# Key tails copied by ScalarE instead of GpSimd, and the denominators' tails as 128-row matmuls

## The chip, the cores and the metric

The kernel runs on one core of a Trainium2 chip. The metric is the device time of one execution in microseconds (us). The kernel before takes 469.25 us (median of three runs, 469.03 to 470.44). Engines are named as in the profile: PE (TensorE, with PEld for its weight loads), DVE (VectorE), ACT (ScalarE), POOL (GpSimd) and SP (the engine that issues all DMAs here).

## The reference

An attention with a soft cap is followed by a gated feed-forward block with a spatial gate. All arrays are float32: batch 4, 12 heads, sequence 448, head size 64, model width 768, hidden width 1024.

```python
scores = scale * q @ k.T                       # scale = 1/8, per head
scores = cap * tanh(scores / cap)              # cap = 30
attn = exp(scores - max(scores)); attn = attn / (sum(attn) + 1e-9)
x = attn @ v                                   # heads side by side: (4, 448, 768)
h = gelu_tanh(x @ w_in); u, v = halves of h    # 512 wide each
v = (v - mean) / sqrt(var + 1e-6) * g_ln       # over the 512
v = einsum('ts,bsd->btd', w_sg, v) + b_sg      # over the sequence
out = x + (u * v) @ w_out
```

## The kernel before

**Pairs and chunks.** Two heads make a pair, six pairs a batch, 24 pairs in all. The 448 keys of a head are three chunks of 128 and a tail of 64. A pair is worked in four steps, one per chunk; chunk 0 is the tail, where the 64 keys of both heads lie on the 128 partitions. From the second pair on the order of chunks is 1, 0, 2, 3, so the tail is the second step of a pair.

**A step.** PE makes the scores (L212, or L198 for a tail) as three products of high and low parts, since each float32 operand is split in two roundings (`hl`, hi by L156 or L158, lo by DVE's subtraction L170). ACT takes the tanh out of PSUM (L225) and the exp in place (L228). PE multiplies the exponentials with v (`pav`, L241), and ACT takes the finished pair out (L249). For the tail, the stationary operand `kt` is block-diagonal: the 64 tail keys of head 0 in one block, of head 1 in the other, zero elsewhere, so that one 128-row matmul makes both heads' scores. Two copies per pair (L173, on POOL) fill the two blocks from `hl`; `kt` has one buffer.

**Denominators.** The sum over keys is a matmul with a column of ones (`den`, L261), always two units at once in a flush; each unit is one chunk of both heads. The four results of a flush go to four groups of 32 rows of one PSUM tile. In batch 0 (`ADDS` = 0) every chunk is a unit: 24 units, 12 flushes, 6 of which hold a tail. A tail's two matmuls contract 64 rows each, taken from partitions 0 to 63 and 64 to 127. In batches 1 to 3 DVE first adds the four chunks of a pair (`presum`, L297), and all units have 128 rows.

**The feed-forward work.** While attention of batch b runs, a generator fills in matmuls of batch b-1: normalisation (L334), the gate half (L368), the other half (L412), the spatial gate (L426), the output (L455). Batch 0 has none to fill in. In its place the weights are decoded in batches 0 and 1: 36 pieces of `w_in` and `w_out` arrive by DMA (L553) and are split into high and low parts by a relay, ACT (L563), DVE (L565, L567, L570, L573), POOL (L575), DVE (L580), ACT or DVE (L158, L156) and POOL (L582). The staging tiles are three in `xu`, and spare `raw` tiles later; `w_sg` (L545, L546) needs four pieces more. Every engine takes its own instructions strictly in the order in which they were laid down by the build's scheduler, which moves them against the program's text by its own estimates.

The end of batch 0's attention is read by ACT (L317), and its reciprocal by DVE (L318, L320 to L322) releases the feed-forward work of batch 0, whose first matmuls are L334.

Of the kernel before, what the change touches and what calls it, by code (L numbers as in the profile page):

```python
# [7 lines left out]
FP32 = mybir.dt.float32  # L8
# [4 lines left out]
ACTF = mybir.ActivationFunctionType  # L13
# [41 lines left out]
def kernel(  # L55
# [15 lines left out]
    nc = tc.nc  # L71
    B, NP, _, S = q2.shape
    NC = w_sgT.shape[1]
    FC = S // 128
    TL = S - 128 * FC
# [8 lines left out]
    wp = ctx.enter_context(tc.tile_pool(name="wp", bufs=1))  # L84
# [16 lines left out]
    wsg = [wp.tile([128, NC, S], FP32R, name=f"wsg{s}") for s in range(2)]  # L101
    sel_r = wp.tile([128, NP, 128], FP32R, name="sel_r")
    rds = wp.tile([128, S], FP32R, name="rds")
    ones_sb = wp.tile([128, NP + 31], FP32, name="ones_sb")
    bsg_sb = wp.tile([128, S], FP32, name="bsg_sb")
    g_sb = wp.tile([128, KF], FP32, name="g_sb")
    cap_sb = wp.tile([128, 1], FP32, name="cap_sb")
# [3 lines left out]
    kt = wp.tile([128, 2, 2 * TL], FP32R, name="kt")  # L111

    def f32(ap):
        return ap.bitcast(FP32)
# [18 lines left out]
    def two(t):  # L133
        return t.rearrange("p (a s) -> p a s", a=2)
# [31 lines left out]
    def prep_b(P):  # L166
        if P >= NPAIR:
            return
        hl = qks[P]
        nc.vector.tensor_tensor(out=hl[:, 1], in0=two(raws[P]), in1=f32(hl[:, 0]), op=ALU.subtract)  # L170
        for h in range(2):
            rows = slice(64 * h, 64 * h + 64)
            nc.gpsimd.tensor_copy(out=kt[rows, :, TL * h:TL * h + TL], in_=f32(hl)[rows, :, 1, 128 * FC:])  # L173
        raw_s.put(raws.pop(P))

    def prep_first():
# [53 lines left out]
    def heads(src, c):  # L230
        if c:
            return [two(src)[:, h, :] for h in range(2)]
        return [src[TL * h:TL * h + TL, :S] for h in range(2)]
# [18 lines left out]
    def den(b, units):  # L252
        if b not in den_t:
            den_t[b] = ps_d.tile([128, 512], FP32, tag="den", name="den")
            units_in[b] = 0
        t = den_t[b]
        for half, (P, c, src) in enumerate(units):
            for h, pr in enumerate(heads(src, c)):
                j = 2 * half + h
                lo, n = (0, 128) if c else (TL * h, TL)  # L260
                nc.tensor.matmul(  # L261
                    out=t[32 * j:32 * j + 32, :S],
                    lhsT=ones_sb[lo:lo + n, NP - 1 - P % NP:NP + 31 - P % NP], rhs=pr,
                    start=(units_in[b] < 2), stop=(units_in[b] >= NP * (NC - ADDS[b]) - 2),
                    skip_group_check=True)
            units_in[b] += 1
# [34 lines left out]
    def flush():  # L301
        b, units = flushes.pop(0)
        den(b, units)
        for u in units:
            raw_s.put(u[2])
        if units_in[b] == NP * (NC - ADDS[b]):
            boost[0] = True
            recip(b)
            later(READY_LAG, set_ready)
# [359 lines left out]
    for g in range(NSTEP + LAG + 2):  # L669
        P, c = divmod(g, NC)  # L670
# [13 lines left out]
        if g < NSTEP:  # L684
            soft2(g)
            if c == 0:
                prep_a(P + 1)
            elif c == 1:
                prep_b(P + 1)
                load_pair(P + 2)  # L690
# [92 lines left out]
```

## Time and profile before

| | |
|---|---|
| median of three runs | 469.25 us |
| the profiled execution's own time | 472.69 us |
| its span, first to last instruction | 470.9 us |
| PE, DVE, ACT, POOL busy | 436.7, 335.7, 283.1, 93.0 us |
| mean granted clock of PE | 0.971 |
| POOL's copies into `kt` | 46, 21.9 us |
| `den` matmul instructions (two for each matmul) | 168, of which 24 with 64 rows |

A matmul's busy time is modelled where matmuls are pipelined, and spans on POOL are rough; the distance from one start to the next is the safer reading. The share of an engine over the whole span mixes stages with different limits, so the stages are read apart.

### The profile page before, as it was taken

The page shows a single profiled execution, that of the slowest core. Times are in us where ns is not written, and L with a number is a line of the kernel's source. Part 1 is how long each engine was busy: PE and PEld are TensorE (multiplying, and loading weights), DVE is VectorE, ACT ScalarE, POOL GpSimd, SP SyncE. Part 2 cuts the span into 40 slices and gives each one's busy share as a digit, 9 for nine tenths or more (in the row PEclk, how much of TensorE's full clock was granted, in tenths as well). Part 3 has the DMA queues.
Part 4 walks back from the last instruction along what each step waited for, and adds up shares of the span by engine and source line. Part 5 has one row for each costly group of instructions (what it writes and reads, how often), then busy time and mean ns, then how long its engine had stood idle before and what let it go on. Part 6 is the DMA issues. An engine that isn't in the chain of part 4 may idle for free.

```text
span 470.9 us, 5916 instructions
## 1 busy us (share of the span) xinstructions
PE 436.7 (93%) x2097; PEld 272.5 (58%) x2097; DVE 335.7 (71%) x621; ACT 283.1 (60%) x420; POOL 93.0 (20%) x143
## 2 busy tenths in 40 slices
PE   5997769879999869999999999999999999899996
PEld 2332223337466536675656666666666576678985
DVE  4859866987999896588587457388596355687662
ACT  4776688974686665538578756636777760044310
POOL 0436644301425543110110101000111000001000
PEclk9999979989999959999999999999999999999999
DMA  7563334221421231231210220420200001200002
GB/s 222 198 197 125 114 120 131 90 84 45 126 67 45 90 107 61 100 99 42 63 39 25 61 61 1 141 91 10 63 22 2 22 2 39 78 1 0 1 27 90
DMA packets 20717, 34.18 MB, mean 73 GB/s; under 512 B 3024, under 2 KB 12880, under 8 KB 20688
## 3 DMA queue, kind: packets, MB, share of 16 engines
q1 hardware_dynamic: 20688, 33.81, 22.8%
q8 instruction: 16, 0.26, 0.3%
q14 instruction: 13, 0.11, 0.1%
HBM read 28.30 MB, written 5.51 MB: 72 GB/s over the span
## 4 chain that ended last, share of the span: by engine, by line
PE 70%; DVE 18%; DMA 3%; POOL 3%; ACT 3%; issue 3%; SPq 0%; POOLq 0%; DVEq 0%; ACTq 0%
PE pav L241 14%; PE gp L455 13%; PE gp L368 11%; PE gp L412 10%; PE sc L212 8%; PE gp L426 8%; DVE raw L297 3%; PE den L261 3%; PE sc L198 2%; DMA xu<-in_w_in_dram 2%; DVE xu L580 2%; PE gp L334 1%; POOL xu L575 1%; ACT raw L225 1%; DVE hl L170 1%
## 5 line engine op out<-in xcount | busy, mean ns | idle before, releaser
L225 ACT ACTIVATE raw<-sc,qsc 128x896 f32<-128x896 f32 (+1 forms) x96 | 86.6, 906 | 36.9 <-PE sc L212 19.1
L241 PE MATMUL pav<-raw,v 128*64 128x448 f32 x384 | 94.1, 576 | 1.0 <-ACT xu L249 1.0
L228 ACT ACTIVATE raw<-raw,cap_sb 128x896 f32<-128x896 f32 (+1 forms) x96 | 90.1, 944 | 1.3
L212 PE MATMUL sc<-hl 64*128 64x448 f32 x432 | 69.6, 418 | 15.0 <-ACT raw L225 15.0
L297 DVE TENSOR_TENSOR raw<-raw,raw 64x448 f32<-64x448 f32 (+1 forms) x72 | 63.2, 878 | 6.1 <-PE pav L241 5.1
L368 PE MATMUL gp<-win,r 128*128 128x512 f32 x264 | 65.3, 398 | 1.3 <-DVE t L357 1.0
L212 PEld LDWEIGHTS sc<-hl 64*128 64x128 f32 x432 | 38.5, 195 | 47.2 <-ACT raw L225 21.5
L412 PE MATMUL gp<-r,win 128*128 128x448 f32 x288 | 65.1, 373 | 0.1
L455 PE MATMUL gp<-r,wout 128*128 128x448 f32 x288 | 63.6, 372 | 0.0
L412 PEld LDWEIGHTS gp<-r,win 128*128 128x128 f32 x288 | 52.7, 188 | 14.5 <-issue 9.6
L455 PEld LDWEIGHTS gp<-r,wout 128*128 128x128 f32 x288 | 53.1, 188 | 11.3 <-issue 3.8
L368 PEld LDWEIGHTS gp<-win,r 128*128 128x128 f32 x264 | 48.2, 188 | 19.5 <-issue 5.6
L241 PEld LDWEIGHTS pav<-raw,v 128*64 128x64 f32 x384 | 25.6, 141 | 52.4 <-issue 41.5
L173 POOL CAST kt<-hl 64x128 fp32r<-64x128 f32 x46 | 21.9, 476 | 155.6 <-PE sc L198 111.3
L426 PE MATMUL gp<-wsg,r 128*128 128x448 f32 x176 | 41.5, 382 | 3.4 <-DVE u L357 3.4
L426 PEld LDWEIGHTS gp<-wsg,r 128*128 128x128 f32 x176 | 33.0, 193 | 14.1 <-issue 6.5
L352 DVE SCALAR_TENSOR_TENSOR t<-t,gp 128x448 f32<-128x448 f32 (+1 forms) x28 | 18.0, 644 | 20.5 <-ACT t L351 20.3
L170 DVE TENSOR_TENSOR hl<-raw,hl 128x896 fp32r<-128x896 f32 x23 | 25.8, 1122 | 8.3 <-ACT hl L158 8.1
L382 POOL TENSOR_TENSOR rs<-rs,pw 128x1 f32<-128x1 f32 (+1 forms) x16 | 9.6, 600 | 109.2 <-DVE rs L381 109.1
L460 DVE TENSOR_TENSOR xu<-xu,gp 128x448 f32<-128x448 f32 x24 | 14.6, 612 | 22.6 <-PE gp L455 22.4
L356 ACT ACTIVATE t<-t 128x448 f32<-128x448 f32 (+2 forms) x32 | 19.3, 604 | 16.9 <-DVE t L352 16.9
L261 PE MATMUL den<-raw,ones_sb 128*32 128x448 f32 (+1 forms) x168 | 29.4, 589 | 0.0
(81 smaller groups left out, 463.7 us busy)
## 6 DMA issues: line engine op xcount, KB each, us to landing
v<-in_vp_dram SPq DMA_DIRECT2D x24, 256.0 KB, 3.0
raw<-in_q_dram SPq DMA_DIRECT2D x24, 224.0 KB, 2.6
raw<-in_k_dram SPq DMA_DIRECT2D x24, 224.0 KB, 3.0
xu<-in_w_in_dram SPq DMA_DIRECT2D x21, 256.0 KB, 2.5
out_dram<-xu SPq DMA_DIRECT2D x24, 224.0 KB, 1.9
raw<-in_w_out_dram SPq DMA_DIRECT2D x11, 256.0 KB, 2.7
u<-in_w_sgT_dram SPq DMA_DIRECT2D x4, 224.0 KB, 5.8
raw<-in_w_in_dram SPq DMA_DIRECT2D x3, 256.0 KB, 3.5
```

Of the source, the lines that this page charges most:

```text
L170: nc.vector.tensor_tensor(out=hl[:, 1], in0=two(raws[P]), in1=f32(hl[:, 0]), op=ALU.subtract)
L173: nc.gpsimd.tensor_copy(out=kt[rows, :, TL * h:TL * h + TL], in_=f32(hl)[rows, :, 1, 128 * FC:])
L212: nc.tensor.matmul(out=sc[:, h, :S], lhsT=hl[rows, w, 1, 128 * c - 128:128 * c], rhs=hl[rows, m, 0], start=(i == 0), stop=(i == 2))
L225: nc.scalar.activation(out=prob(g), in_=src, func=ACTF.Tanh, scale=qsc)
L228: nc.scalar.activation(out=prob(g), in_=prob(g), func=ACTF.Exp, scale=cap_sb)
L241: nc.tensor.matmul(out=pav_t[P][64 * h:64 * h + 64, :S], lhsT=w, rhs=two(p_t[g])[:, h if c else 0, :], start=(g % NC == 0), stop=(c == NC ...
L261: nc.tensor.matmul(out=t[32 * j:32 * j + 32, :S], lhsT=ones_sb[lo:lo + n, NP - 1 - P % NP:NP + 31 - P % NP], rhs=pr, start=(units_in[b] < ...
L297: eng.tensor_tensor(out=a, in0=a, in1=w, op=ALU.add)
L368: yield 1, lambda i=i, c=c, a=a, w=w: nc.tensor.matmul(out=ps, lhsT=a[c][:, t * 128:t * 128 + 128], rhs=win[w][:, c, HF:], start=(i == 0), ...
L412: yield 1, lambda a=a, w=w, c=c, st=st, sp=sp: nc.tensor.matmul(out=ps, lhsT=win[w][:, c, f * 128:(f + 1) * 128], rhs=a[c][:, :S], start=s ...
L426: yield 1, lambda i=i, c=c, a=a, w=w: nc.tensor.matmul(out=ps, lhsT=a[c][:, f * 128:(f + 1) * 128], rhs=wsg[w][:, c, :], start=(i == 0), s ...
L455: yield 1, lambda ps=ps, c=c, a=a, w=w, f=f, st=st, sp=sp: nc.tensor.matmul(out=ps, lhsT=wout[w][:, f, c * 128:(c + 1) * 128], rhs=a[f][:, ...
```

## The change

The two copies into `kt` go from POOL to ACT. The tile of ones grows from one plane to three: plane 0 is as before, planes 1 and 2 hold ones for the partitions of head 0 or head 1 alone. A tail's two denominators then contract all 128 partitions of the tail's exponentials, once with plane 1 and once with plane 2, in place of 64 rows each.

```diff
-    ones_sb = wp.tile([128, NP + 31], FP32, name="ones_sb")
+    ones_sb = wp.tile([128, 3, NP + 31], FP32, name="ones_sb")
...
-            nc.gpsimd.tensor_copy(out=kt[rows, :, TL * h:TL * h + TL], in_=f32(hl)[rows, :, 1, 128 * FC:])
+            nc.scalar.activation(
+                out=kt[rows, :, TL * h:TL * h + TL], in_=f32(hl)[rows, :, 1, 128 * FC:], func=ACTF.Copy)
...
-            for h, pr in enumerate(heads(src, c)):
+            for h in range(2):
                 j = 2 * half + h
-                lo, n = (0, 128) if c else (TL * h, TL)
                 nc.tensor.matmul(
                     out=t[32 * j:32 * j + 32, :S],
-                    lhsT=ones_sb[lo:lo + n, NP - 1 - P % NP:NP + 31 - P % NP], rhs=pr,
+                    lhsT=ones_sb[:, 0 if c else 1 + h, NP - 1 - P % NP:NP + 31 - P % NP],
+                    rhs=two(src)[:, h if c else 0, :],
...
-    ones = _np.zeros((128, NP + 31), _np.float32)
-    ones[:, NP - 1::NP] = 1.0
+    ones = _np.zeros((128, 3, NP + 31), _np.float32)
+    ones[:, 0, NP - 1::NP] = 1.0
+    for h in range(2):
+        ones[TL * h:TL * h + TL, 1 + h, NP - 1::NP] = 1.0
```

The scheduler lays the instructions down anew. In the changed program lines after 173 carry a number higher by one. Three places show what moves.

ACT, the end of batch 0's attention, the twelve instructions up to the one that reads the denominators (L317; `raw` are the exponentials' tiles, `win` the decoded weights), before:

```order
L225 ACTIVATE raw_67<-sc,qsc 128x448
L158 ACTIVATE win_117<-xu 128x256
L228 ACTIVATE raw_67<-raw_67,cap_sb 128x448
L225 ACTIVATE raw_69<-sc,qsc 128x896
L158 ACTIVATE win_117<-xu 128x256
L228 ACTIVATE raw_69<-raw_69,cap_sb 128x896
L249 ACTIVATE xu<-pav 128x448
L563 ACTIVATE xu<-xu 128x256 x2
L225 ACTIVATE raw_70<-sc,qsc 128x896
L563 ACTIVATE raw_72<-raw_72 128x256
L228 ACTIVATE raw_70<-raw_70,cap_sb 128x896
L317 ACTIVATE t_102<-den 64x448
```

The same place in the changed program, from the first copy into `kt` of that pair:

```order
L173 ACTIVATE kt<-hl 64x2x64
L229 ACTIVATE raw_67<-raw_67,cap_sb 128x448
L173 ACTIVATE kt<-hl 64x2x64
L226 ACTIVATE raw_69<-sc,qsc 128x896
L158 ACTIVATE win_117<-xu 128x256
L229 ACTIVATE raw_69<-raw_69,cap_sb 128x896
L250 ACTIVATE xu<-pav 128x448
L564 ACTIVATE xu<-xu 128x256 x2
L226 ACTIVATE raw_70<-sc,qsc 128x896
L158 ACTIVATE win_117<-xu 128x256
L229 ACTIVATE raw_70<-raw_70,cap_sb 128x896
L318 ACTIVATE t_102<-den 64x448
```

The copies stand around the tail's exp, one ahead of it and one behind. Over the whole program up to this point ACT has 14 copies more, and 3 fewer of L563 (14 for 17), 3 fewer of L545 (1 for 4) and 1 fewer of L158 (7 for 8): those come later.

DVE, the same end of batch 0, up to the reciprocal (L318 adds the two halves of the denominators, L320 inverts; `hl` is split for the pair to come), before:

```order
L156 CAST hl<-raw_68 128x896
L567 TENSOR_SCALAR raw_72<-raw_72 128x256
L170 TENSOR_TENSOR hl<-raw_68,hl 128x896
L570 SCALAR_TENSOR_TENSOR raw_72<-raw_72 128x256
L580 TENSOR_TENSOR xu<-xu 128x256
L573 TENSOR_SCALAR raw_72<-raw_72 128x256
L318 SCALAR_TENSOR_TENSOR t_102<-t_102,guard,den 64x448
L297 TENSOR_TENSOR raw_77<-raw_77,raw_67 64x448
L320 RECIPROCAL t_102<-t_102 64x448
```

The same place in the changed program:

```order
L156 CAST hl<-raw_68 128x896
L581 TENSOR_TENSOR xu<-xu 128x256
L170 TENSOR_TENSOR hl<-raw_68,hl 128x896
L581 TENSOR_TENSOR xu<-xu 128x256
L568 TENSOR_SCALAR raw_72<-raw_72 128x256
L571 SCALAR_TENSOR_TENSOR raw_72<-raw_72 128x256
L298 TENSOR_TENSOR raw_77<-raw_77,raw_67 64x448
L319 SCALAR_TENSOR_TENSOR t_102<-t_102,guard,den 64x448
L298 TENSOR_TENSOR raw_77<-raw_77,raw_67 64x448
L321 RECIPROCAL t_102<-t_102 64x448
L574 TENSOR_SCALAR raw_72<-raw_72 128x256
```

Ahead of the addition DVE now has 19 of L565, L567 and L570 each for 21, 18 of L573 for 21 and 18 of L580 for 19, and one of L297 for none. By the eleventh split of a pair (L170, in batch 1) the counts of decode pieces are the same in both programs again.

PE, the second and third flush of batch 0 (`den`; the tiles `raw_72` to `raw_75` are its units, `raw_75` a tail), before:

```order
L212 MATMUL sc<-hl 128x448 x12
L261 MATMUL den<-raw_72,ones_sb 32x448 x2
L261 MATMUL den<-raw_73,ones_sb 32x448 x2
L241 MATMUL pav<-raw_74,v 64x448 x2
L241 MATMUL pav<-raw_75,v 64x448 x2
L198 MATMUL sc<-hl,kt 128x448 x3
L212 MATMUL sc<-hl 128x448 x6
L261 MATMUL den<-raw_74,ones_sb 32x448 x2
L261 MATMUL den<-raw_75,ones_sb 32x448 x2
```

The same in the changed program:

```order
L213 MATMUL sc<-hl 128x448 x6
L261 MATMUL den<-raw_72,ones_sb 32x448
L213 MATMUL sc<-hl 128x448 x6
L261 MATMUL den<-raw_72,ones_sb 32x448
L261 MATMUL den<-raw_73,ones_sb 32x448 x2
L242 MATMUL pav<-raw_74,v 64x448 x2
L242 MATMUL pav<-raw_75,v 64x448 x2
L199 MATMUL sc<-hl,kt 128x448 x3
L261 MATMUL den<-raw_74,ones_sb 32x448
L213 MATMUL sc<-hl 128x448 x6
L261 MATMUL den<-raw_74,ones_sb 32x448
L261 MATMUL den<-raw_75,ones_sb 32x448 x2
```

In these two flushes one of the four matmuls stands apart from the other three, with scores between them. The other ten flushes of batch 0 keep their four side by side.

## Rows read from the trace of the kernel before

**Rows 1.** Busy time of each engine by stage (start:end, length, then engines)
```profile
0.00:22.20 22.20, 16.92 (x63) 6.38 (x63) 14.44 (x38) 12.19 (x15) 5.66 (x14) 1.00 0.68 207
22.20:96.60 74.40, 58.81 (x323) 22.18 (x322) 56.29 (x116) 58.35 (x90) 34.45 (x51) 0.93 0.41 131
96.60:118.00 21.40, 21.36 (x78) 12.36 (x78) 17.09 (x39) 12.46 (x23) 3.12 (x6) 0.92 0.20 59
118.00:172.50 54.50, 46.63 (x227) 28.56 (x226) 51.64 (x105) 38.55 (x66) 25.88 (x33) 0.93 0.32 94
172.50:410.00 237.50, 236.89 (x1153) 154.59 (x1153) 158.31 (x252) 143.69 (x199) 21.70 (x36) 0.99 0.16 49
```
**Rows 2.** Chain that ended last, pieces: start, length, what
```profile
17.12 1.75 PE den L261 x8
22.68 5.12 DMA xu<-in_w_in_dram
68.53 3.27 PE den L261 x8
172.47 2.98 PE gp L426 x7
```
**Rows 3.** Waits in batch 0 after 22.2 us: total, times, longest
```profile
PE sc L212 <- ACT raw L225: 10.3, 7, 2.2
ACT xu L563 <- DMA xu<-in_w_in_dram: 8.2, 6, 2.3
DVE xu L580 <- POOL xu L575: 7.6, 9, 1.3
```
**Rows 4.** Timeline: flushes without and with a tail
```profile
23.56 0.96 PE L261 MATMUL den<-raw,ones_sb 128*32 128x448 f32 x8
27.71 1.82 PE L261 MATMUL den<-raw,ones_sb 128*32 128x448 f32 x8
28.58 0.14 PEld L261 LDWEIGHTS den<-raw,ones_sb 64*32 64x32 f32 x4 [0.73 <-issue]
46.94 1.72 PE L261 MATMUL den<-raw,ones_sb 128*32 128x448 f32 x8
68.46 3.34 PE L261 MATMUL den<-raw,ones_sb 128*32 128x448 f32 x8
```
**Rows 5.** Timeline of ACT: small instructions and the starts behind them
```profile
8.60 0.19 ACT L660 ACTIVATE guard<-guard 128x1 f32<-128x1 f32 x1
8.69 1.00 ACT L225 ACTIVATE raw<-sc,qsc 128x896 f32<-128x896 f32 x1
...
45.37 0.57 ACT L545 ACTIVATE wsg<-u 128x448 fp32r<-128x448 f32 x1
...
62.46 0.42 ACT L158 ACTIVATE win<-xu 128x256 fp32r<-128x256 f32 x1 [1.30 <-DVE xu L580]
62.78 0.42 ACT L563 ACTIVATE xu<-xu 128x256 f32<-128x256 uint32 x1
```
**Rows 6.** DVE's decode in batch 0: all, and two lines (ns min/median/max)
```profile
22.20:96.60 74.40, 38.12 (x93) 0.93 0.41 131
...
L570 DVE SCALAR_TENSOR_TENSOR xu<-xu x17: 411/444/1237, 28.7 to 85.5; 128x256 int32<-128x256 int32 x17
...
L580 DVE TENSOR_TENSOR xu<-xu x16: 410/505/1347, 30.6 to 89.1; 128x256 f32<-128x256 f32 x16
```
**Rows 7.** POOL's copies into kt (L173) in batch 0: busy and count
```profile
22.20:96.60 74.40, 4.39 (x12) 0.93 0.41 131
```
**Rows 8.** Timeline: a pair's lo part on DVE, its tail's tanh on ACT
```profile
54.63 1.08 DVE L170 TENSOR_TENSOR hl<-raw,hl 128x896 fp32r<-128x896 f32 x1
55.99 0.61 ACT L225 ACTIVATE raw<-sc,qsc 128x448 f32<-128x448 f32 x1
...
103.38 0.62 ACT L225 ACTIVATE raw<-sc,qsc 128x448 f32<-128x448 f32 x1
...
109.71 1.08 DVE L170 TENSOR_TENSOR hl<-raw,hl 128x896 fp32r<-128x896 f32 x1
```

## The prediction

> **What bounds the kernel now.** I read the busy time by stage first, then the chain that ended last, then the waits of the stage that the change touches.
>
> By stage [rows 1], the span falls in three. From 172.5 to 410 us PE is busy 236.9 of 237.5 us: nothing counts there but matmuls, and the change takes none away. From 118 to 172.5 us DVE is busy 51.6 of 54.5 us and sets the pace; PE has holes, its clock falls to the lower level near the end (0.93 on the mean of the stage), and the chain re-enters PE at 172.47 us at half clock, seven matmuls in 2.98 us [rows 2]. Batch 0, up to 96.6 us, has no such owner: after 22.2 us PE, DVE and ACT are busy 58.8, 56.3 and 58.4 of 74.4 us. It is a relay. PE waits 10.3 us for ACT's tanh, ACT 8.2 us for weight DMAs, DVE 7.6 us for POOL's product [rows 3]; the chain of waits runs through all of them. What shortens one link shortens batch 0 only when the next link is not late anyway. Then whatever time batch 0 and the DVE-bound stage save together moves the PE-bound stage forward and comes off the end.
>
> **The denominators' tails.** A flush of eight instructions takes 0.96 us when all have 128 rows, 1.82 us with a tail; at half clock 1.72 and 3.34 us [rows 4]. The four 64-row ones do not run beside the others: their weight load starts 0.73 us late [rows 4], as after a change of shape. With 128 rows and masked ones a tail's flush should take what the others take: 0.86 us less at full clock, 1.6 us at half. Batch 0 has six. Two of them lie on the chain, 1.75 us at 17.12 and 3.27 us at 68.53 [rows 2]; they become 0.9 and 1.75 us: -0.9 and -1.5. For the other four I count nothing, since PE waits for ACT behind them; the bound is -0.86 each. Against this, the second and third flush are torn in two, and the matmul that stands apart may cost what the 64-row group cost, 0.86 us each. Neither is on the chain (which is in a weight DMA from 22.68 us [rows 2]): 0, bound +1.7.
>
> **The copies on ACT.** No row shows a copy of 64x128. After a small ACT instruction the next one starts 0.09 us later (128x1) or 0.32 us later (128x256) [rows 5]; half way by width is 0.21, and I take 0.22 us. Fourteen stand ahead of L317: +3.1 us (1.3 to 4.5). The new order takes away ahead of that point three L563 and one L158 at 0.32, and three L545 at 0.47 (0.57 long, less the same 0.10 of overlap [rows 5]): -2.7. Sum +0.4. Does ACT wait for `hl`? Behind the copy stand the tail's exp and the next tanh, for which PE waits. In batch 0 the lo part is done before the tail's tanh is, the nearest by 0.9 us (55.7 against 56.6 [rows 8]). In batch 1 one pair would cost 6.8 us (110.8 against 104.0 [rows 8]), but there the two copies now stand behind the next chunk's tanh and exp and the gate half's first activations. I count 0, bound +2. After 172.5 us 22 copies make 4.8 us in 93.8 us of ACT's idle time [rows 1]: 0.
>
> **What moves on DVE.** Ahead of the reciprocal DVE loses two each of L565, L567 and L570, three L573 and one L580. Ten instructions at the mean of batch 0's decode, 38.12 us for 93 [rows 6], are 4.1 us. It gains an addition of 64x448 that stood just behind, between L580's 0.41 [rows 6] and L170's 1.08 us [rows 8], say 0.6: -3.5 us. DVE is busy 76% of the stage [rows 1], so -2.7 on the path; bounds 0 and -3.5. The 4.1 us come back behind the reciprocal. Between 96.6 and 118 us DVE idles 4.3 of 21.4 us [rows 1] while PE begins the gate half, and part fits there; after that DVE has no room. I take +1.8, near the middle of 0 and +4.1.
>
> **What POOL gives back.** Twelve copies, 4.39 us, leave POOL in batch 0 after 22.2 us [rows 7]. POOL itself is not full, but DVE runs slower beside it: L580 takes 0.41 to 1.35 us, L570 0.41 to 1.24 [rows 6]. The relief lies between nothing and the whole 4.39 us. Since L580's median of 0.51 is only 0.1 above its shortest, most instructions meet no delay, and I take -1.0. Behind 96.6 us eight more copies leave, but three of L546, later in the new order, come: 0.
>
> The Trainium skill ("SBUF — State Buffer", on the ports and their contention) says more: GpSimd and a two-input or two-port VectorE instruction lock each other out for a whole instruction. The spread of L580 agrees with that. By it each copy that meets such an instruction could hold DVE for its full length, and the relief would come near the upper bound, 4.4 us.
>
> The larger tile of ones is 38 KB more in front of the second pair's loads, at 207 GB/s [rows 1] under 0.2 us, hidden under the first pair's work: 0.
>
> **Sum.** Batch 0: -0.9 - 1.5 + 0.4 - 2.7 - 1.0 = -5.7. The DVE-bound stage: +1.8. The rest: 0. Together -3.9 us on an execution of 472.69 us (span 470.9 and 1.8 us around it), 468.8 us. That execution was 3.4 us above the median of the three runs, so the same difference from 469.25 gives 465.4 us. With each doubtful term moved by about half of its bounds the likeliest case runs from 462.5 to 467.8.
>
> **Rivals.**
>
> *ACT becomes the link that holds batch 0: slower.* For it: PE's longest wait there is for ACT's tanh [rows 3], and the copies stand between a tail's exp and the next tanh. Against it: ACT idles 16 us of the 74.4 [rows 1], mostly waiting for decode pieces, and is relieved of seven instructions. If the copies push the tanh each time, the two chain flushes shorten for nothing, twelve copies at 0.32 give +3.8 us, DVE's lighter queue goes into waiting, and the 4.1 us of decode return to the stage where DVE is full, less what fits its idle time. That is +3.8 to +7.9 less POOL's 1.0 to 4.4, 469 to 476 us; I put it at 473. It decides from the point where ACT has no idle time left ahead of a tail's tanh.
>
> *The gains fall into waits: no change.* The relay is held by the weight DMAs and the three staging tiles (8.2 us of ACT's waits [rows 3]). PE's shorter flushes and DVE's lighter queue then end in longer waits: -2.4 from the flushes at most, +1.8 and +0.4 the other way, about 469.
>
> *The relay loosens more than its terms: a larger gain.* The waits in rows 3 (26 us) feed each other; fewer decode pieces per step could free 4 us more of them, POOL's full 4.4 us instead of 1.0 another 3, and if PE no longer idles ahead of 172.5 us its clock is not at half there and another 3 us go. -9 to -11, 459 us. Against it: batch 1's DVE work is unchanged and full.
>
> **How the numbers follow.** My forecast 0.43, the larger gain 0.18, no change 0.16, slower 0.23. About 0.3% (1.4 us) is what a measurement of this kernel can tell from no change. The forecast's small end and the no-change case meet near -1.4 us: faster 0.60, same 0.17, slower 0.23. A range that leaves out a tenth on each side runs from the larger gain, 459, to the middle of the slower case, 473.
>
> **What would show it.** Right: every flush of batch 0 but the two torn ones near 0.96 us (1.7 at half clock); the copies on ACT start the next instruction 0.2 us later, with no wait for `hl` L170 of more than 1 us; the stage up to the first L334 ends near 91 us where it was 96.6; the re-entry of PE's long busy stretch near 168.5 us where it was 172.5; from there the same length. Wrong: an ACT wait for L170 in the chain; the first L334 no earlier; or L334 earlier and the re-entry at the old time, which would say that DVE's stage took all of it back.

## The result and the profile after

The changed kernel takes 466.32 us (median of 13 runs, 464.35 to 468.95) against 469.43 us (13 runs of the kernel before, in turn with it). The ratio is 0.9917, 95% interval [0.989, 0.9943]: 3.9 us less, between 2.7 and 5.2. The forecast's own difference was 3.9 us. The profiled execution lasted 468.95 us, 2.6 us above its median, as that of before lay 3.3 us above the 469.43; so the two traces may be compared directly. Those of the experiments lie at most 2.1 us above their medians: set against the trace of before, they look some 1 to 3 us better than they are.

The span is cut at the first normalisation matmul of batch 0 and at that of the batch after, which PE started at 96.64 and 211.64 us before and at 90.50 and 207.34 us after. Busy time by stage, before (start:end, length, then engines, clock, DMA), with the sum:

```profile
0.00:96.64 96.64, 75.74 (x384) 28.57 (x384) 70.75 (x154) 70.58 (x105) 40.11 (x65) 0.95 0.47 149
96.64:211.64 115.00, 107.13 (x480) 67.10 (x481) 96.60 (x187) 71.75 (x116) 37.03 (x48) 0.93 0.27 82
sum 211.64, PE 182.87 PEld 95.68 DVE 167.35 ACT 142.33 POOL 77.14; mean PE 91.43 PEld 47.84 DVE 83.67 ACT 71.16 POOL 38.57
```

and after:

```profile
0.00:90.50 90.50, 74.06 (x386) 28.87 (x386) 65.23 (x145) 71.49 (x115) 33.15 (x43) 0.92 0.49 159
90.50:207.34 116.84, 106.83 (x478) 67.57 (x479) 99.93 (x196) 77.52 (x134) 43.40 (x42) 0.94 0.27 81
sum 207.34, PE 180.89 PEld 96.44 DVE 165.16 ACT 149.01 POOL 76.55; mean PE 90.44 PEld 48.22 DVE 82.58 ACT 74.51 POOL 38.28
```

Batch 0 is 6.1 us shorter, the stage behind it 1.8 us longer, and from the second cut to the end both need nearly the same (259.3 and 259.8 us; after, PE's granted clock was 0.50 from 407.8 to 411.2 us, where before had 1.00). The second cut is also DVE's busy time plus its idle time up to there: 167.4 + 44.3 before, 165.2 + 42.2 after. Each is about 2 us less. That is a way of counting and names no cause.

In the second stage DVE sets the pace only until PE begins its long busy stretch (the re-entry, at 172.47 us before and 169.29 us after). Busy time up to there and in the 6 us behind it, before:

```profile
96.64:172.47 75.83, 67.96 (x302) 40.88 (x302) 68.68 (x143) 50.94 (x87) 28.99 (x38) 0.93 0.28 84
172.47:178.47 6.00, 6.00 (x13) 2.90 (x13) 3.92 (x12) 2.75 (x5) 0.98 (x1) 0.50 0.01 3
```

and after:

```profile
90.50:169.29 78.79, 68.86 (x296) 41.43 (x296) 68.50 (x147) 53.94 (x97) 34.50 (x34) 0.93 0.26 78
169.29:175.29 6.00, 6.00 (x21) 3.79 (x22) 4.97 (x11) 4.86 (x11) 1.91 (x2) 0.75 0.10 37
```

Up to the re-entry the stage is 3.0 us longer after, and DVE's busy time is the same: all of it is idle time of DVE, 10.3 us for 7.2. From the re-entry to the second cut it is 1.1 us shorter (38.05 us for 39.17). PE is busy there throughout in both, and in the first 6 us its granted clock was 0.50 before and 0.75 after. DVE's longest wait ahead of the re-entry (total, times, longest), before and then after:

```profile
DVE t L352 <- ACT t L351: 2.2, 1, 2.2
```

```profile
DVE xu L581 <- POOL xu L576: 4.5, 1, 4.5
```

The denominators' flushes answer to [rows 4]; timeline of PE after, the second flush (torn in two), the fifth and the ninth of the stretch:

```profile
22.68 0.94 PE L261 MATMUL den<-raw,ones_sb 128*32 128x448 f32 x2
24.73 0.95 PE L261 MATMUL den<-raw,ones_sb 128*32 128x448 f32 x6
...
37.84 0.96 PE L261 MATMUL den<-raw,ones_sb 128*32 128x448 f32 x8
...
62.19 1.72 PE L261 MATMUL den<-raw,ones_sb 128*32 128x448 f32 x8
```

Whole flushes take 0.96 us, with a tail or without, and 1.72 at the lower clock; the two torn ones take 0.94 + 0.95. The copies on ACT, timeline after, answer to [rows 5]:

```profile
48.01 0.62 ACT L226 ACTIVATE raw<-sc,qsc 128x448 f32<-128x448 f32 x1
48.73 0.31 ACT L173 ACTIVATE kt<-hl 64x128 fp32r<-64x128 f32 x1
48.94 0.65 ACT L229 ACTIVATE raw<-raw,cap_sb 128x448 f32<-128x448 f32 x1
49.62 0.31 ACT L173 ACTIVATE kt<-hl 64x128 fp32r<-64x128 f32 x1
49.95 1.01 ACT L226 ACTIVATE raw<-sc,qsc 128x896 f32<-128x896 f32 x1
```

The next instruction starts 0.21 and 0.33 us behind a copy's start. ACT's waits for the split over the whole execution (total, times, longest):

```profile
ACT kt L173 <- DVE hl L170: 1.4, 2, 0.8
```

The chain that ended last, pieces after (start, length, what), answers to [rows 2]:

```profile
17.70 0.89 PE den L261 x8
73.15 0.89 PE den L261 x8
...
100.36 0.47 ACT wsg L546
100.90 1.22 POOL wsg L547
102.12 0.54 issue
102.68 1.65 issue
104.33 1.16 POOL wsg L547
105.49 0.69 POOL win L583
106.18 1.11 POOL wsg L547
...
111.77 3.78 PE gp L369 x8
...
169.29 2.98 PE gp L427 x7
```

The first flush of batch 0 is on the chain in both, 1.75 us before and 0.89 after. The other that before has there, at 68.53 us, is the ninth. After, the ninth is the one at 62.19 us: 1.72 us for 3.34, at half clock (granted 0.50) in both, and no longer on the chain. The 0.89 at 73.15 us is the eleventh. New on the chain is POOL between 100 and 107 us: the three `wsg` subtractions that the new order put behind batch 0. The timeline of POOL there,

```profile
100.90 4.58 POOL L547 TENSOR_TENSOR wsg<-u,wsg 128x448 fp32r<-128x448 f32 x2 [10.94 <-ACT wsg L546]
105.45 0.73 POOL L583 TENSOR_TENSOR win<-raw,win 128x256 fp32r<-128x256 f32 x1
106.14 1.15 POOL L547 TENSOR_TENSOR wsg<-u,wsg 128x448 fp32r<-128x448 f32 x1
```

and what DVE does next:

```profile
107.90 0.82 DVE L581 TENSOR_TENSOR xu<-xu 128x256 f32<-128x256 f32 x1 [4.55 <-POOL xu L576]
```

DVE stands still 4.55 us for a decode product that queues behind them on POOL. POOL itself had stood idle for 10.94 us until ACT's rounding (L546) released the first of them. PE's re-entry, seven matmuls in 2.98 us, is still at half clock and comes 3.2 us earlier.

### The profile page after: what moved, and what is told of

Its sections match the earlier page's. It is cut to its first block, busy times and chain, and to the rows that moved or that the text cites. A ratio compares the mean times of both kernels' runs of the same rounds, so it can differ in the third digit from the quotient of the medians.

```text
span 467.2 us, 5885 instructions
## 1 busy us (share of the span) xinstructions
PE 435.6 (93%) x2097; PEld 274.4 (59%) x2097; DVE 333.5 (71%) x621; ACT 293.1 (63%) x466; POOL 83.1 (18%) x97
## 4 chain that ended last, share of the span: by engine, by line
PE 70%; DVE 13%; issue 5%; POOL 4%; DMA 4%; ACT 3%; SPq 0%; POOLq 0%; DVEq 0%; ACTq 0%
PE pav L242 13%; PE gp L456 13%; PE gp L369 12%; PE gp L413 10%; PE sc L213 9%; PE gp L427 7%; PE den L261 2%; DVE raw L298 2%; DMA xu<-in_w_in_dram 2%; PE sc L199 2%; PE gp L335 1%; ACT raw L226 1%; POOL win L583 1%; DVE hl L170 1%; DVE xu L581 1%
## 5 line engine op out<-in xcount | busy, mean ns | idle before, releaser
L242 PE MATMUL pav<-raw,v 128*64 128x448 f32 x384 | 93.0, 574 | 2.1 <-ACT xu L250 2.1
L369 PE MATMUL gp<-win,r 128*128 128x512 f32 x264 | 68.1, 411 | 3.3 <-DVE t L358 3.3
L298 DVE TENSOR_TENSOR raw<-raw,raw 64x448 f32<-64x448 f32 (+1 forms) x72 | 64.3, 894 | 6.1 <-PE pav L242 5.1
L213 PEld LDWEIGHTS sc<-hl 64*128 64x128 f32 x432 | 38.7, 196 | 43.6 <-issue 17.9
L369 PEld LDWEIGHTS gp<-win,r 128*128 128x128 f32 x264 | 50.7, 197 | 21.3 <-issue 4.9
L383 POOL TENSOR_TENSOR rs<-rs,pw 128x1 f32<-128x1 f32 (+1 forms) x16 | 10.3, 646 | 244.7 <-DVE rs L382 244.6
L170 DVE TENSOR_TENSOR hl<-raw,hl 128x896 fp32r<-128x896 f32 x23 | 26.4, 1149 | 7.5 <-ACT hl L158 7.4
L261 PE MATMUL den<-raw,ones_sb 128*32 128x448 f32 x168 | 26.5, 570 | 0.6 <-DVE raw L298 0.6
L583 POOL TENSOR_TENSOR win<-xu,win 128x256 fp32r<-128x256 f32 x21 | 19.8, 943 | 32.4 <-ACT win L158 17.8
```

Source lines behind the costliest of these rows:

```text
L213: nc.tensor.matmul(out=sc[:, h, :S], lhsT=hl[rows, w, 1, 128 * c - 128:128 * c], rhs=hl[rows, m, 0], start=(i == 0), stop=(i == 2))
L242: nc.tensor.matmul(out=pav_t[P][64 * h:64 * h + 64, :S], lhsT=w, rhs=two(p_t[g])[:, h if c else 0, :], start=(g % NC == 0), stop=(c == NC ...
L261: nc.tensor.matmul(out=t[32 * j:32 * j + 32, :S], lhsT=ones_sb[:, 0 if c else 1 + h, NP - 1 - P % NP:NP + 31 - P % NP], rhs=two(src)[:, h ...
L298: eng.tensor_tensor(out=a, in0=a, in1=w, op=ALU.add)
L369: yield 1, lambda i=i, c=c, a=a, w=w: nc.tensor.matmul(out=ps, lhsT=a[c][:, t * 128:t * 128 + 128], rhs=win[w][:, c, HF:], start=(i == 0), ...
L583: nc.gpsimd.tensor_tensor(out=dst[1], in0=f, in1=f32(dst[0]), op=ALU.subtract)
```

## The experiments

First what the kernels say side by side. "Pieces" are the 256-wide decode instructions that DVE has ahead of batch 0's reciprocal in its order; the two cuts, and DVE's busy and idle time up to the second, are from each kernel's profiled execution.

| kernel | median us | ratio [95%] | pieces | first cut | second cut | DVE busy + idle |
|---|---|---|---|---|---|---|
| before | | 1 | 117 | 96.6 | 211.6 | 167.4 + 44.3 |
| after | 466.32 | 0.9917 [0.989, 0.9943] | 107 | 90.5 | 207.3 | 165.2 + 42.2 |
| e1 masked only | 468.43 | 0.9968 [0.9937, 0.9998] | 117 | 94.1 | 207.5 | 167.3 + 40.2 |
| e2 ACT only | 469.38 | 0.9982 [0.9954, 1.001] | 107 | 90.1 | 207.6 | 165.0 + 42.6 |
| e3 ACT twice | 463.41 | 0.9858 [0.9809, 0.9906] | 96 | 82.4 | 201.7 | 162.6 + 39.1 |
| e4 POOL kept | 469.31 | 0.9974 [0.9946, 1.0001] | 107 | 91.1 | 208.5 | 167.2 + 41.3 |
| e5 before, pace 8 | 465.54 | 0.9902 [0.9866, 0.9937] | 93 | 86.6 | 205.7 | 163.0 + 42.8 |
| e6 after, pace 8 | 465.76 | 0.9902 [0.9863, 0.9941] | 87 | 83.1 | 205.6 | 162.0 + 43.6 |
| e7 masked, pace 8 | 465.29 | 0.9908 [0.9872, 0.9943] | 93 | 87.1 | 206.2 | 162.4 + 43.8 |
| e8 after, pace 6 | 459.84 | 0.9787 [0.9749, 0.9824] | 79 | 82.1 | 199.5 | 163.8 + 35.7 |
| e9 masked, pace 6 | 465.04 | 0.9892 [0.9869, 0.9914] | 91 | 88.7 | 204.9 | 164.6 + 40.3 |
| e10 ACT only, pace 6 | 461.82 | 0.9823 [0.98, 0.9846] | 79 | 84.2 | 201.1 | 164.1 + 37.0 |
| e11 POOL kept, pace 6 | 460.99 | 0.9818 [0.9794, 0.9841] | 79 | 81.9 | 200.1 | 165.1 + 35.0 |
| e12 after, pace 5 | 466.46 | 0.993 [0.9895, 0.9964] | 76 | 80.7 | 207.7 | 160.4 + 47.3 |

Each row's ratio is to runs of the kernel before made with it; e1 to e4, e5 to e8, and e9 to e12 were run together.

**e1: the masked denominators alone.** The kernel before with the larger tile of ones, the copies left on POOL; the order on every engine is that of before.

```diff
-                lo, n = (0, 128) if c else (TL * h, TL)
...
+                    lhsT=ones_sb[:, 0 if c else 1 + h, NP - 1 - P % NP:NP + 31 - P % NP],
+                    rhs=two(src)[:, h if c else 0, :],
```

> The masked tails alone; POOL keeps the copies, and the order of all instructions on all engines is that of the kernel before. My sum: the two flushes on the chain shorten, -2.4 us, time to before 0.994 to 0.996, all flushes of batch 0 near 0.96 us. Rival, the new order made the gain: shorter flushes end in longer waits, 0.998 to 1.000. Rival, the masked tails are all of it: 0.990 to 0.993.

Measured 0.9968 [0.9937, 0.9998]: 1.5 us less, 0.1 to 3.0. That is between the range of the sum and that of the waits; the interval leaves out the third, that the tails are all of it. The tails have a worth of their own, smaller at the centre than the -2.4 of the sum, which lies inside the interval.

**e2: the copies alone.** ACT copies, tails as 64-row matmuls; the order is that of the changed kernel.

```diff
-            nc.gpsimd.tensor_copy(out=kt[rows, :, TL * h:TL * h + TL], in_=f32(hl)[rows, :, 1, 128 * FC:])
+            nc.scalar.activation(
+                out=kt[rows, :, TL * h:TL * h + TL], in_=f32(hl)[rows, :, 1, 128 * FC:], func=ACTF.Copy)
```

> The copies on ACT alone; tails keep 64 rows, and the order on all engines is that of the changed kernel. My sum without the flushes: -2.4 in batch 0's rest and +1.8 behind it and no more than 1 of relief, about -1.5 us, 0.995 to 0.999. Rival, the new order made the gain: -3.5, 0.991 to 0.994. Rival, the masked tails are all of it, the copies on ACT cost what they free: 1.000 to 1.003.

Measured 0.9982 [0.9954, 1.001]: 0.8 us less, not told from no change. It lies in the range of the sum, and the interval leaves out the larger gain by the new order. The two parts alone add up to -0.5%, the change has -0.83%; the difference of 1.6 us is within the three intervals, so whether the parts help each other stays open.

**e3: each copy on ACT made twice.**

```diff
-            nc.scalar.activation(
-                out=kt[rows, :, TL * h:TL * h + TL], in_=f32(hl)[rows, :, 1, 128 * FC:], func=ACTF.Copy)
+            for _ in range(2):
+                nc.scalar.activation(
+                    out=kt[rows, :, TL * h:TL * h + TL], in_=f32(hl)[rows, :, 1, 128 * FC:], func=ACTF.Copy)
```

> The changed kernel with each copy on ACT made twice (46 copies more; the order moves more decode pieces behind the reciprocal, 17 of L565's kind ahead of it for 19). If ACT has room (my sum), 0.2 us for each of 12 in batch 0, partly taken by idle time: +0 to +2 us on the changed kernel, 0.991 to 0.996 to before. If ACT holds batch 0 (rival): +4 us and more, 1.000 or above.

Measured 0.9858, outside both ranges: by the ratios 2.8 us faster than the changed kernel, with intervals that overlap slightly (0.989 to 0.9906). More work on ACT, and no more time: that speaks against the slower rival, for which ACT holds batch 0. But the run was not the clean test it was meant as: the scheduler answered the extra copies by moving 11 more decode pieces behind the reciprocal. That made a new theory: the number of pieces ahead of the reciprocal is the lever, and the copies' engine matters mainly because it moves them.

**e4: POOL's old copies made as well,** into a tile that nobody reads. PE and ACT keep the changed kernel's order, DVE's differs in a few places, and as many pieces lie ahead of the reciprocal.

```diff
+    kx = wp.tile([128, 2, TL], FP32R, name="kx")
...
+            nc.gpsimd.tensor_copy(out=kx[rows], in_=f32(hl)[rows, :, 1, 128 * FC:])
```

> The changed kernel with POOL making its old copies as well, into a tile nobody reads; PE's and ACT's orders are those of the changed kernel. It gives POOL's relief alone. My sum: +1 us in batch 0, little behind it, 0.993 to 0.995 to before. By a full lock of DVE for each copy, +4 in batch 0: 0.999 to 1.002. No relief at all: 0.990 to 0.993.

Measured 0.9974, between the range of the sum and that of a full lock: 0.57% or 2.7 us of the gain is gone (the intervals of the two kernels just fail to overlap). Busy times of e4 over its two stages:

```profile
sum 208.48, PE 180.82 PEld 96.00 DVE 167.15 ACT 148.82 POOL 82.45; mean PE 90.41 PEld 48.00 DVE 83.57 ACT 74.41 POOL 41.23
```

and POOL's copies alone (`kx`) in the same stretch (busy, count, clock, DMA):

```profile
0.00:208.48 208.48, 9.59 (x28) 0.94 0.37 114
```

DVE, with the same instructions, has 2.0 us more than after (167.15 for 165.16). The 28 copies are 9.6 us long, though POOL has only 5.9 us more than after, since its other work is shorter; so they cost DVE about a fifth of their own length. The kernels at this pace divide in the same way: with POOL's copies DVE has 167.2 to 167.4 us (before, e1, e4), without them 165.0 and 165.2 (e2, after). Since DVE's order in e4 is not quite that of the changed kernel, the 2.7 us are POOL's relief only as far as those places don't matter. The Trainium skill ("SBUF — State Buffer", on its two separate sides) says that the port pair of VectorE and GpSimd is an exclusive lock and the loser blocks for the whole instruction; the direction agrees, and the size is a fifth of what it would be if every copy blocked DVE for its whole length.

**e5 to e8: the decode paced slower,** one constant that sets how many pieces of the weights are due by the end of batch 0, in the kernel before (e5), the changed one (e6, e8) and e1 (e7).

```diff
-PRO = 12
+PRO = 8
```

(6 in e8.)

> The kernel before with one constant changed: the weights' decode is paced slower (PRO 12 to 8). Ahead of batch 0's reciprocal DVE has 93 of its 256-wide pieces where the kernel before has 117; ACT's count there stays at 25. Nothing of the change under study is in it. Theory A (decode pieces on DVE hold batch 0's relay and cost less behind it, which is what the run with doubled copies gained by): a ratio of 0.985 to 0.992 to the kernel before, the first normalisation matmul 8 to 12 us earlier. Theory B (that run gained by the copies being off POOL and not by the order of the decode): 0.998 to 1.002. Theory C (the DVE-bound stage takes all of it back): the first normalisation matmul earlier by as much as in A, the second batch's at the old time, 0.998 to 1.002.

> The changed kernel with the same slower pace (PRO 8): 87 pieces ahead of the reciprocal where the changed kernel has 107 and the one with doubled copies 95. Theory A: 0.982 to 0.988. Theory B: about 0.992, as the changed kernel. Theory C: about 0.992, with an earlier first normalisation.

> The masked denominators alone, with POOL's copies kept, at the slower pace (PRO 8). Theory A: between the kernel before and the changed kernel at that pace, 0.3% below the first (the tails' own worth). If the copies on ACT are worth more than their order of the decode, it stays 0.5% or more above the changed kernel at that pace; if their worth was the order alone, the two agree within 0.2%.

> The changed kernel at a still slower pace (PRO 6): 79 pieces ahead of the reciprocal. Theory A: 0.98 to 0.985 while batch 1 has room for the pieces. If the weights then come too late for the gate half, PE idles between its matmuls behind the first normalisation, and the ratio is 0.99 or above.

e5 has nothing of the change in it and gains as much (0.9902): theory A holds there, theory B falls. 24 pieces fewer bring its first cut forward by 10.1 us, of which the difference of the two executions from their medians could be 2: 0.33 to 0.42 us each, against a mean busy time of 0.41 [rows 6]. The stage behind it took back 4.2 us, 0.17 per piece. e7 equals e5, so the 0.3% expected of the tails is not seen at that pace. It also agrees with e6, as expected if the copies on ACT are worth their order alone; with intervals of 0.35% to each side neither is shown. e6 missed its 0.982 to 0.988: its first cut is 3.4 us ahead of e5's and its second at the same place. There theory C was right. DVE's longest waits in that second stage, e6 (total, times, longest):

```profile
DVE raw L581 <- POOL raw L576: 6.1, 4, 4.5
DVE xu L338 <- PE gp L335: 4.4, 4, 2.1
DVE hl L170 <- ACT hl L158: 2.6, 1, 2.6
```

and in e8:

```profile
DVE t L393 <- POOL rs L383: 1.9, 4, 0.6
DVE raw L581 <- POOL raw L576: 1.9, 4, 0.7
DVE t L319 <- ACT t L318: 1.3, 1, 1.3
```

e8 is the fastest kernel of all, 459.84 us, 2.1% under before and beyond what theory A gave it: not its first cut (1 us ahead of e6's) but its second stage is shorter (117.4 us for 122.5), and DVE is idle there for 7.7 us where e6 has 18.6.

**e9 to e12: the parts at pace 6, and pace 5.** e9 is e1, e10 is e2 and e11 is e4, each with the constant at 6; e12 is the changed kernel with 5.

```diff
-PRO = 12
+PRO = 6
```

> The masked denominators with POOL's copies into kt, pace 6. Its order is nearly that of pace 8 (91 decode pieces ahead of the reciprocal on DVE for 93). Theory A (what counts is how many pieces lie ahead of the reciprocal, and the copies on ACT are worth as much as the pieces they make the scheduler move): as at pace 8, 0.988 to 0.992. Rival (the pace by itself gave the changed kernel at pace 6 its time): 0.979 to 0.983.

> Copies on ACT, tails as 64-row matmuls, pace 6: ACT's and DVE's order that of the changed kernel at pace 6. If the tails still are worth 1.5 to 2.4 us there: 0.982 to 0.984. If they have become slack with the relay loosened: 0.978 to 0.980.

> The changed kernel at pace 6, with POOL's old copies made as well, into a tile that nobody reads. The end of the DVE-bound stage is DVE's busy plus its idle time up to there; at pace 12 the same copies on POOL lengthened DVE's busy time by 2.1 us. If that holds at this pace: 0.983 to 0.985, DVE's busy time 2 us longer than without them. If POOL's copies are hidden here: 0.978 to 0.980.

> The changed kernel at pace 5: 76 decode pieces ahead of the reciprocal for 79 at pace 6. Theory A: 0.975 to 0.980, DVE idle less than 36 us in all up to the second batch's normalisation. If the turning point is passed (the later pieces now hold the gate half): 0.982 to 0.988.

e9 stays at 0.9892: its order kept 91 pieces ahead, and the pace by itself gave nothing more. e11, run beside it, is 4.1 us faster although POOL still makes all its copies: what separates the two is that `kt` is filled by ACT and the order that comes with it (79 pieces). e10 and e11 lie 0.3 to 0.4% above e8, e10 in the range expected if the tails keep their worth, e11 between its two ranges; but their intervals overlap with e8's, so at this pace neither is shown. DVE's busy time up to the second cut, e8 and then e11:

```profile
sum 199.46, PE 178.41 PEld 94.18 DVE 163.78 ACT 150.67 POOL 70.96; mean PE 89.21 PEld 47.09 DVE 81.89 ACT 75.33 POOL 35.48
```

```profile
sum 200.12, PE 177.62 PEld 93.68 DVE 165.09 ACT 150.48 POOL 78.15; mean PE 88.81 PEld 46.84 DVE 82.54 ACT 75.24 POOL 39.07
```

POOL's copies, 9.4 us of them here, cost DVE 1.3, for the 2 that were expected.

e12, at 0.993, missed theory A's 0.975 to 0.980 and even the 0.982 to 0.988 given for a turning point that is passed. It has the earliest first cut of all (80.7), and the longest second stage (127.0 us). So the count of pieces goes with the length of batch 0, not strictly (e9, with 91, ends it later than e7 with 93), and not with the whole. Two places in that stage, both on e12's chain; timeline of e12, POOL:

```profile
123.49 2.33 POOL L383 TENSOR_TENSOR rs<-rs,pw 128x1 f32<-128x1 f32 x1 [0.88 <-DVE rs L382]
125.79 0.87 POOL L583 TENSOR_TENSOR win<-raw,win 128x256 fp32r<-128x256 f32 x1
...
131.09 3.33 POOL L583 TENSOR_TENSOR win<-xu,win 128x256 fp32r<-128x256 f32 x1 [2.73 <-ACT win L158]
134.39 0.72 POOL L583 TENSOR_TENSOR win<-raw,win 128x256 fp32r<-128x256 f32 x1
135.08 0.60 POOL L576 TENSOR_TENSOR raw<-raw 128x256 f32<-128x256 f32 x1
```

and DVE at the second of them:

```profile
131.41 0.28 DVE L568 TENSOR_SCALAR raw<-raw 128x256 int32<-128x256 int32 x1
131.61 1.08 DVE L170 TENSOR_TENSOR hl<-raw,hl 128x896 fp32r<-128x896 f32 x1
132.62 0.41 DVE L571 SCALAR_TENSOR_TENSOR raw<-raw 128x256 int32<-128x256 int32 x1
132.95 0.68 DVE L358 SCALAR_TENSOR_TENSOR t<-t,t 64x512 f32<-64x512 f32 x1
133.55 0.28 DVE L574 TENSOR_SCALAR raw<-raw 128x256 int32<-128x256 int32 x1
133.75 0.68 DVE L380 BATCH_NORM_STATS2 st<-t 64x6 f32<-64x512 f32 x1
135.72 0.43 DVE L581 TENSOR_TENSOR raw<-raw 128x256 f32<-128x256 f32 x1 [1.28 <-POOL raw L576]
```

While DVE runs without a gap, a subtraction on POOL lasts 3.33 us where the next takes 0.72. It ends as DVE's run ends, and then DVE stands still 1.28 us for the POOL product queued behind it. So read, the two engines hold each other up in turn: DVE packed full makes POOL late, and a late POOL makes DVE idle. The second half is shown by the wait; the first is argued from the times alone, since most subtractions of this trace during which DVE was busy throughout took 0.73 to 1.14 us. Of the 9.6 us by which e12's second stage is longer than e8's, 7.4 are idle time of DVE; how much of that comes from such places was not shown.

## Why the prediction was right, point by point

- **The whole and the stages: right in the times.** -6.1 us in batch 0 (forecast -5.7), +1.84 behind it (+1.8), +0.6 from there on (0). First L335 at 90.5 (near 91), re-entry at 169.29 (near 168.5). That the +1.84 meets the +1.8 is luck: it is 3.0 us more of DVE's idle time ahead of the re-entry, less 1.1 us behind it, where the lower clock lasted less long.
- **The tails: right in the row, large in the sum.** Every whole flush is at the price of the others. The first lost 0.86 us and the ninth 1.62, still at half clock, as forecast (-0.9, -1.5); but the ninth has left the chain. Alone (e1) they bring 1.5 us, for -2.4. The torn flushes cost nothing on the chain.
- **The copies on ACT: right.** Next start 0.20 to 0.33 us later in most (0.22), no wait for L170 over 0.8 us (none over 1), and a kernel with twice as many was no slower (e3, in another order).
- **The pieces moved on DVE: right in batch 0, wrong in what comes back.** I priced ten of them at 0.76 of their busy time. e5 measures 0.33 to 0.42 us each, 0.8 to 1 of it. For the way back I said that DVE has no room. DVE's busy time up to the re-entry did not grow (68.50 us for 68.68); its idle time did. e1 and e4 have the same tails and both have copies on POOL; between them, with the copies on ACT and their order, the first cut gains 3.0 us and the second loses 1.0, so about 4 came back there, for the 1.8 I took.
- **POOL's relief: the term that was mis-sized.** I took -1.0, since L580's median was only 0.1 us above its shortest. e4 measures 2.7 us in the time and 2.0 in DVE's busy time. No single line of DVE carries it: from the changed kernel to e4 the largest increase of a group is 0.8 us (the casts into `win`), so a reading by two lines, as mine was, could not find it. The full 4.4 us was not reached in DVE's busy time.
- **The three `wsg` pieces: the step that failed.** I set eight copies leaving POOL behind 96.6 us against three of them coming, and counted 0. A copy took 0.37 us [rows 7]; two of the subtractions took 4.58, and DVE lost 4.55 us behind them. After, e2 and e4, which have the three pieces there, all show the wait of 4.5 us; before and e1 have none over 2.2 us up to the re-entry. So what I put down to DVE's lack of room was, in that stretch, mostly POOL's queue. An order without them there was not run by itself.

The sum came out by luck. By the ratios the steps from before to e1 (the tails), from e1 to e4 (the copies on ACT and their order, with copies still on POOL) and from e4 to the changed kernel (POOL's relief) are -1.5, +0.3 and -2.7 us; my terms for them were -2.4, -0.5 (0.4 - 2.7 + 1.8) and -1.0. POOL's relief was taken 1.7 us too small, and the other two 0.9 and 0.8 too favourable. Each step is uncertain by some 1.4 to 1.9 us, so the middle one is not told from zero. The rival of the larger gain was right that the relay can loosen further: it did in e3, e5 and e8, with still more pieces moved. But the count alone does not do it: the changed kernel with 87 pieces (e6) gains nothing measurable over its 107, and with 76 (e12) it is no faster either.

Left open: why the order at pace 6 gives DVE so few waits (e8, e10 and e11 all have it: 35 to 37 us idle), and the one at pace 8 does not. At pace 8 the change is worth nothing measurable (e5 and e6 at 0.9902), at pace 12 it is worth 0.83%; at pace 6 the copies on ACT with their order are worth 1.1% (e9 to e8). It has no price of its own apart from the order it is scheduled into.

## What to carry to other kernels

Where a scheduler lays instructions down anew, list first what moved across the point that releases the next stage, and price that along with the edit's own instructions. Here what moved shortened one stage and lengthened the next by at least as much (e1 to e4), while a pacing constant alone gained as much as the edit (e5), and another value of it together with the edit 2.1% (e8). For an engine that paces a stage, account for the stage's end as its busy plus its idle time: an edit that frees it early helps only if its later waits don't grow (after, e6, e12). An engine that is 36% busy (POOL's 77.1 of 211.6 us before) can still tax the pacing one: its copies lengthened DVE's work by up to a fifth of their own length, and three subtractions moved into DVE's stage made DVE wait 4.55 us.

## What the runs showed of the hardware

- In e12 a POOL product of one column (128x1, L383) took 2.33 us at 123.49 us while DVE ran instruction after instruction, and 0.55 to 0.56 us in its other eleven executions; a POOL subtraction of 128x256 took 3.33 us, the next 0.72. A busy DVE alone does not decide it: at 118.2 us the product took 0.56 us with DVE 92% busy beside it.
- Small copies on POOL (64x128) went with more busy time on DVE, by a fifth of their own length (2.0 for 9.6 us, e4), in another order by a seventh (1.3 for 9.4, e11).
- Matmuls with 128 rows, half of the ones zero, cost the same as those with ones throughout, and a flush with a tail 0.86 us less than with 64-row ones [rows 4]. The Trainium skill ("TensorEngine Tiling (Array Packing)", key properties) says that a change of tiling mode drains the array; the 0.73 us by which the 64-row group's weight load came late, most of that 0.86, fit it.
